# Joint stores in the last batch, a deferred matmul in its first block product, and a wider spread of the second batch's row transposes

## The chip, the core and the metric

The kernel runs on one core of one Trainium2 chip. Five engines work side by side, each through its own instruction stream: TensorE (PE, matmuls and transposes; its weight loads are listed as PEld), VectorE (DVE), ScalarE (ACT), GpSimd (POOL) and SyncE (SP, which here only issues DMAs). They meet through semaphores. The metric is device time in microseconds (us) of one launch, the median of several runs; lower is better.

## The reference

Retention attention with a decay per head, then a Fourier mix with a feed-forward block behind it. There are 4 batches of 768 rows, 8 heads of 64 columns (512 together), and a hidden width of 2048.

```python
gamma = 1.0 - 2.0 ** (-5.0 - np.arange(H, dtype=np.float32))
for t in range(S):
    state = gamma[None, :, None, None] * state + np.einsum('bhd,bhe->bhde', k[:, :, t], v[:, :, t])
    y[:, :, t] = scale * np.einsum('bhd,bhde->bhe', q[:, :, t], state)
...
X = np.fft.fft(x, axis=1)
X = np.fft.fft(X, axis=2)
u = x + np.real(X).astype(np.float32)
mu = np.mean(u, axis=-1, keepdims=True)
var = np.mean((u - mu) ** 2, axis=-1, keepdims=True)
un = (u - mu) / np.sqrt(var + 1e-06)
ch = np.maximum(un @ w_ch1, 0.0) @ w_ch2
return (u + ch).astype(np.float32)
```

## The kernel before

The batches are numbered 0 to 3. Each goes through the same stages. Attention works on pairs of heads: casts of q, k and v on POOL (`cast_unit`, L378 to L393), transposes of q and k, a masked product `wkA` (L605), the states `wkK` (L624, whose matmuls read the cast v that L393 writes), and the output `wkY` (L655, L659). The Fourier mix has two steps: `s1_unit` (L741, evicted by ACT at L748 and reversed by DVE at L752) and `s2_unit`. `s2_unit(b, kb)` makes one block `kb` of 128 rows (0 to 5) of `u`: four short matmuls into a tile `pq` (L838), two copies on ACT (L840, L841), two operations on DVE (L845, L848), two additions on POOL (L875, L877). `norm_unit` takes the row statistics on DVE (L895, L896). In batches 0 to 2 ACT then writes the centred rows `un` in half precision (L900), and the scale 1/sqrt(var) is applied behind the second matrix (`rstd_unit`, L932 and L934). In batch 3 `root_unit` (ACT, L910) and `scaled_unit` (DVE, L917, L918) write the fully normalised rows. `unT_unit` transposes `un`: for batch 0 and the first three row blocks of batch 1 on PE through PSUM (L945, evicted at L950 by DVE or at L952 by ACT), for all later ones by a DMA transpose that SP issues (L941). The tile `un` has two buffers, so the third row block's `un` takes the buffer of the first.

The feed-forward block of batches 1 and 2 works on halves of three row blocks: 16 units `h_unit` (four matmuls of 384 columns each, L961; evicted by ACT at L965 or DVE at L967 as `ACT_ROWS` says) give the hidden rows, and three `ch_unit` of 16 matmuls of 512 columns (L1000) give the result, which DVE finishes at L1004 and SP stores at L1008. Both take their PSUM tiles from a pool of three (`ps_pm`); nearly everything else takes them from a pool of five (`ps_g`).

The last batch is done in three groups `p` of two row blocks. In each, eight `h3_unit` (L1043) make the hidden rows of 256 rows, two hidden blocks n and n+8 per unit, evicted by ACT (L1048) or, for n = 4, DVE (L1050). Then `p3_unit` makes the second matrix product by blocks with seven products instead of eight, each of eight matmuls (f = 0 to 7) of 256 columns (L1107). Product 1 (bank "a") is copied by ACT into `w` (L1118); product 2 is accumulated on top of it in the same bank. Products 5, 6, 7 and 3 read sums of hidden blocks (`hsum`, four DVE operations at L1067 behind units n = 3 and n = 7). Both f = 7 of product 1 and f = 7 of product 4 read what the unit n = 7 wrote. `PROD` gives the order of the products, one for groups 0 and 1 and one for group 2. The results go to two tiles `ob` of a pool of three, and each is stored with a DMA of its own.

What sets the order: `streams` is a list of (units, start, end) with times in batches, `emit` spaces each list evenly and sorts all units by due time. Below time 3.0 the program is handed to a scheduler that may reorder within limits; above it the order is pinned as written. Due times of the first three row blocks of the next batch come from `DA0` (after batch 0) and `DA1`: entries 2 and 3 are for the `s2_unit` list, entries 4 and 5 for the `unT_unit` list. For batch 3 `mix_units` puts `norm_unit`, `root_unit` and `scaled_unit` behind each `s2_unit` in one list of 12.

Of the kernel before, what the change touches and what calls it, by code (L numbers as in the profile page):

```python
# [13 lines left out]
f32 = mybir.dt.float32  # L14
# [4 lines left out]
P = 128  # L19
B, H, S, D = 4, 8, 768, 64  # L20
DM = 512
DFF = 2048
NCH = S // P
# [9 lines left out]
DM0, DM1 = (0.120, 0.208, 0.265, 0.344), (0.004, 0.137, 0.232, 0.341)  # L33
TS0 = (0.249, 0.368, 0.406, 0.410, 0.479, 0.544, 0.680, 0.685)
TS1 = (-0.040, -0.020, 0.048, 0.585)
DA0, DA1 = (0.068, 0.080, 0.173, 0.203, 0.315, 0.321), (0.063, 0.067, 0.063, 0.158, 0.168, 0.189)
LD0, LD1 = (0.172, 0.226), (-0.370, 0.140)
HT0 = (0.655, 0.675, 0.673, 0.628)
NPE = 2
# [1 line left out]
        (0.345, 0.415, 0.435, 0.460, 0.500))  # L41
WS = (0.6, 0.97)
H3_ACT = (0, 1, 2, 3, 5, 6, 7)
PROD = ((1, 4, 2, 5, 6, 7, 3), (1, 4, 6, 7, 5, 2, 3))
HS_AT = {3: (0, 4), 7: (4, 8)}
ACT_ROWS = ((2, 5, 6, 7, 8, 9, 10, 14), (0, 3, 6, 7, 9, 10, 11, 12, 14, 15))

# [2 lines left out]
def kernel(  # L50
# [9 lines left out]
    nc = tc.nc  # L60
# [3 lines left out]
    def pool(name, bufs, **kw):  # L64
        return ctx.enter_context(tc.tile_pool(name=name, bufs=bufs, **kw))
# [11 lines left out]
    up = pool("up", 2)  # L77
    qnp = pool("qnp", 1)
    hp_ = pool("hp", 1)
    obp = pool("obp", 3)  # L80
    stt = pool("stt", 2)
    ps_g = pool("ps_g", 5, space=PSUM)
    first = ExitStack()
# [14 lines left out]
    last = const.tile([P, 4], f32, tag="last")  # L98
# [894 lines left out]
    def ch_unit(b, rt, rb3, part):  # L993
        def run():
            rb = rt * 3 + rb3
            if part == 0:
                psc_of[0] = ps_pm.tile([P, DM], f32, tag="pm", name="psc")
            psc = psc_of[0]
            for fb in range(4 * part, 4 * part + 4):
                nc.tensor.matmul(psc, ht16[:, fb, rb3 * P:(rb3 + 1) * P], w216[:, fb, :],  # L1000
                                 start=(fb == 0), stop=(fb == NFB - 1))
            if part == 3:
                ob = obp.tile([P, DM], f32, tag="ob", name="ob")
                nc.vector.scalar_tensor_tensor(out=ob, in0=psc, scalar=lb[b]["st"][:, rb, 3:4],  # L1004
                                               in1=lb[b]["u"][:, rb, :], op0=ALU.mult,
                                               op1=ALU.add)
                for c0, c1 in ((0, 256), (256, DM)) if b == 0 else ((0, DM),):
                    nc.sync.dma_start(out[b, rb * P:(rb + 1) * P, c0:c1], ob[:, c0:c1])  # L1008
        return run

    def wsum_unit(j, hi):
# [22 lines left out]
    ws, pr, hs = {}, {}, {}  # L1034
# [35 lines left out]
    def p3_unit(p, n):  # L1070
        def run():
            u = lb[B - 1]["u"]
            r0, r1 = 2 * p, 2 * p + 1
            u11, u12 = u[:, r0, 0:256], u[:, r0, 256:DM]
            u21, u22 = u[:, r1, 0:256], u[:, r1, 256:DM]
            end = p == 2
            if n == 1:
                pr.clear()
                pr["o"] = [obp.tile([P, DM], f32, tag="ob", name="ob") for _ in range(2)]
                pr["w"] = inp.tile([P, 2, NCH, D], f32, tag="in32", name="ws32").rearrange(  # L1080
                    "p a c d -> p (a c d)")[:, 0:256]
            o0, o1 = pr["o"]
            o11, o12, o21, o22 = o0[:, 0:256], o0[:, 256:DM], o1[:, 0:256], o1[:, 256:DM]
            w = pr["w"]
            bank, first, last, lh, rh = {
                1: ("a", True, False, lambda f: ht16[:, f, 0:P], lambda f: w216[:, f, 0:256]),
                2: ("a", False, True, lambda f: ht16[:, 8 + f, 0:P],
                    lambda f: w216[:, 8 + f, 0:256]),
                3: ("d", False, True, lambda f: hs[3][:, f], lambda f: w216[:, 8 + f, 256:DM]),
                4: ("e", True, True, lambda f: ht16[:, 8 + f, P:256], lambda f: wsum(3, f)),  # L1090
                5: ("d", True, False, lambda f: hs[0][:, f], lambda f: wsum(0, f)),
                6: ("b", True, True, lambda f: hs[1][:, f], lambda f: wsum(1, f)),
                7: ("c", True, True, lambda f: hs[2][:, f], lambda f: wsum(2, f))}[n]
            cols = ((0, 128), (128, 256)) if bank == "d" and end else ((0, 256),)
            if first:
                pr[bank] = [ps_g.tile([P, 256], f32, tag="g", name="psc", padded_shape=[P, DM])
                            for _ in cols]

            def add(o, x, y):
                nc.vector.tensor_tensor(out=o, in0=x, in1=y, op=ALU.add)  # L1100

            def store(r, c0, c1, src, queue=nc.sync):
                queue.dma_start(out[B - 1, r * P:r * P + P, c0:c1], src)

            for ps, (c0, c1) in zip(pr[bank], cols):
                for f in range(8):
                    nc.tensor.matmul(ps[:, c0:c1], lh(f), rh(f)[:, c0:c1],  # L1107
                                     start=first and f == 0, stop=last and f == 7,
                                     skip_group_check=True)
                if n == 3:  # L1110
                    add(o12[:, c0:c1], ps[:, c0:c1], u12[:, c0:c1])
                    if end:
                        store(r0, 256 + c0, 256 + c1, o12[:, c0:c1], nc.sync if c0 else nc.scalar)
                elif n == 5:
                    add((o22 if end else u22)[:, c0:c1], ps[:, c0:c1], u22[:, c0:c1])
            ps = pr[bank][0]
            if n == 1:
                nc.scalar.copy(w, ps)  # L1118
            elif n == 2:
                add(o11, ps, u11)  # L1120
                if end:
                    store(r0, 0, 256, o11)
            elif n == 4:
                add(u21, ps, u21)
            elif n == 6:
                add(w, ps, w)
                if end:
                    add(u22, u22, w)
                    nc.gpsimd.tensor_tensor(out=u21, in0=u21, in1=w, op=ALU.add)
                else:  # L1130
                    x = u[:, r1].rearrange("p (t m) -> p t m", t=2)
                    nc.gpsimd.tensor_tensor(out=x, in0=x, in1=w.unsqueeze(1).to_broadcast(
                        [P, 2, 256]), op=ALU.add)
                nc.gpsimd.tensor_tensor(out=u12, in0=u12, in1=w, op=ALU.add)
            elif n == 7:
                add(u22 if end else o22, ps, u22)
                add(o21, ps, u21)
                if end:
                    store(r1, 0, 256, o21)
                else:  # L1140
                    store(r1, 0, DM, o1)
            if n == 3 and not end:
                store(r0, 0, DM, o0)
            elif n == 5 and end:
                store(r1, 256, DM, o22)
        return run
# [100 lines left out]
    def mix_units(b, kbs):  # L1247
        s2s = [s2_unit(b, kb) for kb in kbs]
        if b == B - 1:
            s2s = [u for kb, s2 in zip(kbs, s2s) for u in (  # L1250
                s2, norm_unit(b, kb), root_unit(kb), scaled_unit(kb))]
        return s2s, [unT_unit(b, kb) for kb in kbs]

# [23 lines left out]
    streams = []  # L1277
    for b in range(B):
# [19 lines left out]
        if b < B - 1:  # L1298
            s2s, unTs = mix_units(b, [3, 4, 5])
# [7 lines left out]
        if b + 1 < B:  # L1307
            steps = attn_steps(b + 1)
            if b == 0:
                streams.append(([load_unit(1, i, 6) for i in range(4)], LD0[0], LD0[1]))  # L1310
                streams.append(([qt_zeros], 0.1, 0.15))
                streams.append(([half_tables], HT0[0], HT0[1]))
                streams.append(([pad_unit], HT0[2], HT0[3]))
                ts = TS0
            else:
                streams.append(([load_unit(b + 1, i) for i in range(4)], b + LD1[0], b + LD1[1]))
                n = [len(u) for u in steps[1:]]
                ts = list(TS1[:2]) + [TS1[2] + TS1[3] * sum(n[:j]) / sum(n) for j in range(6)]
            streams.append((steps[0], b + ts[0], b + ts[1]))
            streams += [(u, b + ts[j + 2], b + ts[j + 3]) for j, u in enumerate(steps[1:])]  # L1320
            end = b + ts[-1]
            da = DA0 if b == 0 else DA1
            streams.append(([s1_unit(b + 1, e, cb) for cb in range(2) for e in range(2)
                             if cb or b + 1 >= FB], end + da[0], end + da[1]))
            s2s, unTs = mix_units(b + 1, [0, 1, 2])
            streams += [(s2s, end + da[2], end + da[3]), (unTs, end + da[4], end + da[5])]
            if b + 1 == B - 1:
                streams.append(([wsum_unit(j, hi) for j in range(4) for hi in range(2)],
                                b + WS[0], b + WS[1]))
# [31 lines left out]
```

## Time and profile before

| what | value |
|---|---|
| median of 3 runs (lowest, highest) | 245.66 us (245.02, 246.42) |
| the profiled execution's own time | 245.43 us |
| span of its instructions | 243.4 us |
| what lies around the span | 2.03 us |
| PE busy, share of the span | 231.2 us, 95% |
| DVE busy | 192.5 us, 79% |
| ACT busy | 126.7 us, 52% |
| POOL busy | 87.7 us, 36% |
| granted PE clock in every stretch | 1.00 |
| last matmuls, modelled end | 240.15 us |

The page of the profile is read from the top: busy times, then the span in slices, then the chain of waits that ended last. The timeline lists instructions in order of time: start, duration, engine, source line, operation, output and inputs, shapes, count, and in brackets how long the engine stood idle before it and what ended that. Rows of the same kind that follow each other are merged, so a row `x8` covers eight instructions. Starts of matmuls are measured and their ends are modelled: two matmuls overlap in the list by some 0.2 us, and a stall shorter than that shows only as a longer distance from start to start. Those distances are therefore what the text works with.

### The profile page before, as it was taken

How to read it: one execution, taken by the hardware profiler on the slowest of the kernel's cores; microseconds unless marked ns; L12 is line 12 of the kernel's file. 1: busy time of each engine (PE TensorE's matmuls, PEld its weight loads, DVE VectorE, ACT ScalarE, POOL GpSimd, SP SyncE). 2: the span in 40 equal slices, each digit the busy share in tenths (PEclk: the TensorE clock that was granted, in tenths of full speed). 3: DMA queues.
4: the chain of work that ended last, by engine and by line, in shares of the span. 5: the costliest groups of instructions: out<-in, count | busy, mean ns of one | idle time of the engine just before them, and what ended most of it. 6: DMA issues, size and time to landing. Idle time of an engine off the chain costs nothing.

```text
span 243.4 us, 5668 instructions
## 1 busy us (share of the span) xinstructions
PE 231.2 (95%) x2160; PEld 155.6 (64%) x2160; DVE 192.5 (79%) x478; ACT 126.7 (52%) x280; POOL 87.7 (36%) x150
## 2 busy tenths in 40 slices
PE   5798899999999998999999999999999999999994
PEld 2354668956676655665567546565567458888884
DVE  8998957897797888996887777899986846776274
ACT  8798669588675434652237523741247306253330
POOL 7776601465600057791000554680002402330302
PEclk9999999999999999999999999999999999999999
DMA  7999999699989768997999767887100231131202
GB/s 171 253 264 147 195 203 205 154 252 231 287 188 226 134 142 163 166 208 114 247 284 214 163 120 222 126 112 170 67 22 0 46 109 43 24 109 24 86 3 88
DMA packets 100363, 36.41 MB, mean 150 GB/s; under 512 B 89968, under 2 KB 98288, under 8 KB 100336
## 3 DMA queue, kind: packets, MB, share of 16 engines
q1 hardware_dynamic: 95968, 31.79, 62.3%
q0 software_dynamic: 4224, 4.19, 10.7%
q8 instruction: 17, 0.28, 0.5%
q14 instruction: 10, 0.08, 0.1%
q10 hardware_dynamic: 144, 0.07, 0.1%
HBM read 27.26 MB, written 6.29 MB: 138 GB/s over the span
## 4 chain that ended last, share of the span: by engine, by line
PE 71%; DMA 7%; ACT 7%; DVE 6%; SPq 4%; POOL 2%; issue 2%; ACTq 0%; POOLq 0%; DVEq 0%
PE psc L1000 21%; PE psh L961 19%; PE psh L1043 9%; PE psc L1107 8%; DMA k<-in_k_dram 5%; SPq L171 4%; PE wkA L605 3%; PE ps L741 3%; DMA q<-in_q_dram 2%; PE wkY L659 2%; PE pq L838 2%; PE wkY L655 1%; ACT un L891 1%; PE wkK L624 1%; DVE bst L895 1%
## 5 line engine op out<-in xcount | busy, mean ns | idle before, releaser
L1000 PE MATMUL psc<-w,ht 128*128 128x512 f16 x288 | 68.2, 379 | 0.0
L961 PE MATMUL psh<-unT,w 128*128 128x384 f16 x320 | 59.7, 326 | 0.0
L875 POOL TENSOR_TENSOR u<-u,x 128x256 f32<-128x256 f32 x21 | 13.4, 637 | 105.6 <-DVE u L845 97.4
L1000 PEld LDWEIGHTS <-ht 128*128 128x128 f16 x288 | 27.2, 98 | 26.1 <-issue 0.2
L961 PEld LDWEIGHTS <-w 128*128 128x128 f16 x320 | 29.8, 98 | 15.9 <-issue 0.7
L965 ACT ACTIVATE ht<-psh 128x384 f16<-128x384 f32 x46 | 22.3, 490 | 23.6 <-PE psh L961 23.3
L608 DVE TENSOR_TENSOR atm<-wkA,maskp 128x512 f16<-128x512 f32 x36 | 23.8, 682 | 1.4 <-PE wkA L605 1.4
L1043 PE MATMUL psh<-unT,w 128*128 128x256 f16 x192 | 21.5, 273 | 0.0
L895 DVE BATCH_NORM_STATS2 bst<-u 128x6 f32<-128x512 f32 x21 | 14.6, 694 | 7.0 <-POOL u L877 6.5
L1043 PEld LDWEIGHTS <-w 128*128 128x128 f16 x192 | 18.7, 98 | 2.2
L967 DVE TENSOR_SCALAR ht<-psh 128x384 f16<-128x384 f32 x34 | 18.6, 548 | 1.8 <-PE psh L961 1.7
L1048 ACT ACTIVATE ht<-psh 128x512 f16<-128x512 f32 x21 | 12.5, 597 | 13.6 <-PE psh L1043 7.9
L634 DVE SCALAR_TENSOR_TENSOR s<-s,gk,wkK 128x128 f16<-128x128 f16 x48 | 16.4, 341 | 3.0 <-ACT s L630 2.2
L1004 DVE SCALAR_TENSOR_TENSOR ob<-psc,stats,u 128x512 f32<-128x512 f32 x18 | 13.4, 743 | 5.8 <-PE psc L1000 5.8
L900 ACT ACTIVATE un<-u,stats 128x512 f16<-128x512 f32 x15 | 10.8, 722 | 12.1 <-DVE stats L896 7.9
L667 ACT ACTIVATE x<-wkY,gexp 128x384 f16<-128x384 f32 x24 | 12.8, 581 | 8.0 <-PE wkY L659 8.0
L388 POOL TENSOR_SCALAR kd<-k,gexp 128x384 f16<-128x384 f32 x24 | 13.9, 588 | 4.3 <-DMA k<-in_k_dram 4.3
L157 PE MATMUL wps<-ht 128*128 128x512 f16 x40 | 12.6, 418 | 2.2 <-POOL ht L208 2.2
L877 POOL TENSOR_TENSOR u<-u,x 128x256 f32<-128x256 f32 x21 | 13.5, 644 | 3.0 <-DVE stats L896 3.0
L605 PE MATMUL wkA<-qTz,kT 128*128 128x256 f16 x72 | 13.4, 272 | 0.1
L840 ACT COPY qn<-pq 128x128 f32<-128x128 f32 x18 | 4.9, 273 | 14.2 <-PE pq L838 14.2
L978 PE MATMUL psh<-unT,w 128*128 128x128 f16 x192 | 11.5, 219 | 0.1
(189 smaller groups left out, 421.2 us busy)
## 6 DMA issues: line engine op xcount, KB each, us to landing
q<-in_q_dram SPq DMA_DIRECT2D x16, 384.0 KB, 6.0
k<-in_k_dram SPq DMA_DIRECT2D x16, 384.0 KB, 5.6
v<-in_v_dram SPq DMA_DIRECT2D x16, 384.0 KB, 6.2
w<-in_moe_w_ch_dram POOLq DMA_DIRECT2D x8, 512.0 KB, 11.0
out_dram<-ob SPq DMA_DIRECT2D x16, 256.0 KB, 2.4
out_dram<-ob SPq DMA_DIRECT2D x15, 128.0 KB, 1.9
unT<-un SPq DMA_TRANSPOSE x15, 2.4
qTz<-q16z SPq DMA_TRANSPOSE x8, 4.5
```

Source lines behind the costliest of these rows:

```text
L388: kc = nc.gpsimd.tensor_scalar(out=kd[:, :, h2, :], in0=k32[:, h2], scalar1=gkd[:, h0 + h2:h0 + h2 + 1], scalar2=1.0, op0=ALU.mult, op1=AL ...
L605: mm = nc.tensor.matmul(wk[:, c2], st["kT"][:, c, :], st["qT"][:, :, c, :], start=True, stop=True)
L608: nc.vector.tensor_tensor(out=st["atm"][:, 2 * part:2 * part + 2], in0=wk, in1=maskp[:, PAIR_ORDER[i]].unsqueeze(1).to_broadcast([P, 2, 2, ...
L634: nc.vector.scalar_tensor_tensor(out=s16[:, c], in0=s16[:, c - 1], scalar=gk2[:, hp:hp + 1], in1=wk[:, c - c0], op0=ALU.mult, op1=ALU.add)
L877: nc.gpsimd.tensor_tensor(out=u[:, kb, 256:512], in0=u[:, kb, 256:512], in1=x[:, kb, 1, 257:1:-1], op=ALU.add)
L895: nc.vector.bn_stats(bst, u[:, kb, :])
L961: nc.tensor.matmul(psh, w116[:, cb, fb * P:(fb + 1) * P], unT[:, cb, rt * 384:(rt + 1) * 384], start=(cb == 0), stop=(cb == 3))
L965: nc.scalar.activation(ht16[:, fb, :], psh, AF.Relu, bias=0.0, scale=-1.0)
L967: nc.vector.tensor_scalar(out=ht16[:, fb, :], in0=psh, scalar1=-1.0, scalar2=0.0, op0=ALU.mult, op1=ALU.max)
L1000: nc.tensor.matmul(psc, ht16[:, fb, rb3 * P:(rb3 + 1) * P], w216[:, fb, :], start=(fb == 0), stop=(fb == NFB - 1))
L1043: nc.tensor.matmul(psh[:, t], w116[:, cb, fb * P:(fb + 1) * P], unT[:, cb, p * 256:(p + 1) * 256], start=(cb == 0), stop=(cb == 3))
L1107: nc.tensor.matmul(ps[:, c0:c1], lh(f), rh(f)[:, c0:c1], start=first and f == 0, stop=last and f == 7, skip_group_check=True)
```

## The change

There are four edits.

1. `DA0`: the transposes of batch 1's first three row blocks are due from 0.292 to 0.326 instead of 0.315 to 0.321 behind the attention's end.
2. `mix_units` for batch 3 puts three empty units ahead of its list, and the list's end is moved so that the spacing stays; each unit of batch 3's first three row blocks is due three places later.
3. `p3_unit`: for product 1 only f = 0 to 6 are made at first; f = 7 is kept as a function and made just ahead of f = 7 of product 4, with the copy to `w` behind it. `PROD` for groups 0 and 1 takes product 5 ahead of product 2.
4. Results of the last batch go to one tile `o32` of 6 row blocks, in the pool and under the tag of `u`; groups 0 and 1 store both row blocks with one DMA at the end of product 3 (before: one after product 7, one after product 3). Batch 0's results, stored before as two halves of 256 columns, are stored with one DMA per row block.

```diff
-DA0, DA1 = (0.068, 0.080, 0.173, 0.203, 0.315, 0.321), (0.063, 0.067, 0.063, 0.158, 0.168, 0.189)
+DA0, DA1 = (0.068, 0.080, 0.173, 0.203, 0.292, 0.326), (0.063, 0.067, 0.063, 0.158, 0.168, 0.189)
...
-PROD = ((1, 4, 2, 5, 6, 7, 3), (1, 4, 6, 7, 5, 2, 3))
+PROD = ((1, 4, 5, 2, 6, 7, 3), (1, 4, 6, 7, 5, 2, 3))
...
-                for c0, c1 in ((0, 256), (256, DM)) if b == 0 else ((0, DM),):
-                    nc.sync.dma_start(out[b, rb * P:(rb + 1) * P, c0:c1], ob[:, c0:c1])
+                nc.sync.dma_start(out[b, rb * P:(rb + 1) * P, :], ob)
...
             if n == 1:
-                pr.clear()
-                pr["o"] = [obp.tile([P, DM], f32, tag="ob", name="ob") for _ in range(2)]
+                if p == 0:
+                    pr["o"] = up.tile([P, NCH, DM], f32, tag="u32", name="o32")
...
-            o0, o1 = pr["o"]
+            o0, o1 = pr["o"][:, r0], pr["o"][:, r1]
...
+            if n == 1:
+                pr["late"] = lambda: nc.tensor.matmul(pr["a"][0], lh(7), rh(7), start=False,
+                                                      stop=False, skip_group_check=True)
             for ps, (c0, c1) in zip(pr[bank], cols):
                 for f in range(8):
-                    nc.tensor.matmul(ps[:, c0:c1], lh(f), rh(f)[:, c0:c1],
-                                     start=first and f == 0, stop=last and f == 7,
-                                     skip_group_check=True)
+                    if f < 7 or n != 1:
+                        if f == 7 and n == 4:
+                            pr["late"]()
+                            nc.scalar.copy(w, pr["a"][0])
+                        nc.tensor.matmul(ps[:, c0:c1], lh(f), rh(f)[:, c0:c1],
+                                         start=first and f == 0, stop=last and f == 7,
+                                         skip_group_check=True)
...
-            if n == 1:
-                nc.scalar.copy(w, ps)
-            elif n == 2:
+            if n == 2:
...
-                else:
-                    store(r1, 0, DM, o1)
             if n == 3 and not end:
-                store(r0, 0, DM, o0)
+                nc.sync.dma_start(out[B - 1, r0 * P:r0 * P + 256].rearrange(
+                    "(r p) m -> p r m", p=P), pr["o"][:, r0:r0 + 2])
...
-            s2s = [u for kb, s2 in zip(kbs, s2s) for u in (
+            s2s = [lambda: None] * 3 + [u for kb, s2 in zip(kbs, s2s) for u in (
                 s2, norm_unit(b, kb), root_unit(kb), scaled_unit(kb))]
...
-            streams += [(s2s, end + da[2], end + da[3]), (unTs, end + da[4], end + da[5])]
+            streams += [(s2s, end + da[2], end + da[2] + (da[3] - da[2]) * len(s2s) / (
+                3 if b + 1 < B - 1 else 12)), (unTs, end + da[4], end + da[5])]
```

## The prediction

> **What bounds the kernel now.** First the page: the busy times (PE 231.2 of 243.4), then its summary of the chain that ended last.
>
> ```profile
> PE 71%; DMA 7%; ACT 7%; DVE 6%; SPq 4%; POOL 2%; issue 2%; ACTq 0%; POOLq 0%; DVEq 0%
> ```
>
> PE is busy nearly throughout, and the chain runs along it from about 61 us to 240 us. No matmul is added or removed, so the change can only win what PE loses standing still. I went through the distances of matmul starts in the timeline and found three places that the edits touch. The first is the hand-over from batch 0 to batch 1 (timeline, start and duration in us):
>
> ```profile
> 93.06 0.30 ACT L932 ACTIVATE stats<-stats,epsT 128x3 f32<-128x3 f32 x1 [0.79 <-DVE stats L896]
> ...
> 93.33 0.61 PE L945 MATMUL pst<-ident,un 128*128 128x128 f16 x8
> ...
> 93.83 0.72 ACT L900 ACTIVATE un<-u,stats 128x512 f16<-128x512 f32 x1 [0.47 <-PE pst L945]
> 94.15 0.83 POOL L393 TENSOR_SCALAR v<-v 128x768 f16<-128x768 f32 x1
> ...
> 94.61 0.40 PE L945 MATMUL pst<-ident,un 128*128 128x128 f16 x4 [0.67 <-ACT un L900]
> 94.84 0.40 PE L838 MATMUL pq<-gk,g16r 128*128 128x129 f16 x4
> 95.08 0.44 PE L624 MATMUL wkK<-v,kd 128*128 128x128 f16 x5
> ```
>
> Eight transposes take 0.44 (93.33 to 93.77), and the next four start at 94.61: 0.84 lost. `un` of the third row block (L900) waits in turn for the first block's transposes, whose buffer it takes. The second place is batch 3's first `s2_unit`, in batch 2's time:
>
> ```profile
> 184.99 0.63 PE L838 MATMUL pq<-gk,g 128*128 128x129 f16 x3
> ...
> 185.33 0.11 PEld L838 LDWEIGHTS <-g 128*128 128x128 f16 x2 [0.32 <-ACT g L748]
> ...
> 185.46 0.65 PE L961 MATMUL psh<-unT,w 128*128 128x384 f16 x3
> ...
> 186.00 0.98 PE L961 MATMUL psh<-unT,w 128*128 128x384 f16 x5
> ```
>
> From 184.99 to 186.00 lie four pq matmuls (0.24, as the unit at 188.34 with its successor at 188.58) and three L961 (0.65 per four in the chain, so 0.49): 0.73 of work in 1.01, so 0.28 lost to ACT's copies of `g`. The third place is product 1 of the last batch, in groups 0 and 1:
>
> ```profile
> 207.04 1.03 PE L1107 MATMUL psc<-w,ht 128*128 128x256 f16 x8
> ...
> 220.40 1.20 PE L1107 MATMUL psc<-w,ht 128*128 128x256 f16 x8
> ...
> 221.30 1.75 PEld L1107 LDWEIGHTS <-ht 128*128 128x128 f16 x17 [0.26 <-ACT ht L1048]
> 221.43 1.04 PE L1107 MATMUL psc<-wsum,ht 128*128 128x256 f16 x8
> ```
>
> Group 0 needs 0.87 from product 1 (207.04) to product 4 (207.91), group 1 needs 1.03; group 2 repeats it (233.68 to 234.71). So 0.16 is lost twice, waiting for the unit n = 7.
>
> **Part 3, the deferred matmul.** In the built program PE makes 7 + 7 matmuls, then the deferred one, then product 4's last. ACT ends the n = 7 eviction 0.86 after product 1 starts (220.66 + 0.60 against 220.40); the first matmul that reads it now comes after 14 x 0.109 = 1.52. That wait is gone in groups 1 and 2; in group 0 there was none. What is late next is the copy to `w`: it moves from the end of product 1 to about 1.63 + 0.24 = 1.87 behind its start and ends at 2.24. Product 2 overwrites that bank at 24 x 0.109 = 2.61 in groups 0 and 1 because product 5 now stands between; in group 2 the sum with `w` follows product 6, which ends at 2.61 + 0.17. Product 5's first reading of n = 7's `hsum` comes at 20 x 0.109 = 2.18, and that sum is ready at 221.71 - 220.40 = 1.31. Gain **0.32**, bounds 0 (something else ends at the same time) and 0.32.
>
> **Part 2, three places later.** PE now makes two h units between the last L741 and the first pq, 1.30 of work, while ACT's last copy of `g` is done 0.80 after L838's old start (183.65 + 2.14). The stall of 0.28 goes. New order behind: two h units, pq, two h units, pq, one h unit, pq, L1000. Each h unit waits for an eviction that I placed by hand: the tightest is L1000, which takes the tile of the fourth h unit. That unit ends at 187.81, ACT evicts it from about 188.0 to 188.5, and PE comes to L1000 at 188.9. Gain **0.28**, bounds 0.28 and a loss (rival three). The DMA transposes of batch 3's rows go out later; their cover is worked out there.
>
> **Part 1, transposes spread.** PE now makes 24 L1000 (from 87.29, 0.216 each, to 92.47), eight transposes (to 92.91), the last four L1000 (to 93.77), then the four late transposes. The `un` they need is bound by ACT alone: L932 starts at 93.06 because the third row's statistics end at 93.02, it takes 0.30, L900 0.72, and PE follows 0.06 later as now (94.55 to 94.61): 94.14, against 94.61. So 0.37 of the stall stays. Behind stand four pq matmuls (0.24 with the 0.23 of transposes: 94.61) and L624, which reads the cast v that POOL ends at 94.15 + 0.83 = 94.98. PE waits there 0.41 to 95.02, where it now arrives at 95.08 and never notices. Then five L624 (0.28) and the whole next `s2_unit`'s four pq (0.24) bring L961 to 95.54, against 95.52 now. What is won is three pq matmuls (0.17) that today stand behind 20 L961 and then stand ahead of them. Against this DVE's order changes: L895 of the fourth row block, which waits for POOL, now stands ahead of the second h unit's eviction L967. I get that eviction at 97.66 to 98.2, and the fifth h unit, which takes its tile, would start at 98.15: about 0.10 lost. Net gain **0.05**. Upper bound: if L624 does not wait, L961 is bound by DVE's L950 (PSUM transposed at 94.55, DVE busy with L1004 to 94.65, 0.41, PE 0.05 later: 95.11 to 95.13): 0.39 + 0.17 = 0.56. Lower bound: one h unit's time (0.65) of further stall behind L895: -0.55.
>
> [...]
>
> **Part 4, stores and buffer: 0.** The joint store of group 0 leaves at the old second store's time (215.25); the next DMA on SP, a row transpose at 215.63 that landed at 218.04, is needed by group 2 at 226.67: 8.6 of cover. Group 1's leaves near 228.2; two stores took 2.0 to 2.3 us each there, so it lands by 232.6 at the worst, and the next store is at 238.68. `o32` takes batch 2's `u`, last read by L1004 at 199.79 + 0.75, first written near 210. Batch 0's six stores save SP 0.42 each; SP's rows there wait for DVE's results, and no PE wait of 60 to 180 us in the list of waits names a DMA. Bounds: -0.2 (one longer transfer ahead of a load) to +0.4 (one issue).
>
> **Sum.** 0.32 + 0.28 + 0.05 = 0.65. The profiled execution took 245.43 (243.4 and 2.03 around it): 244.78. It lies 0.23 below the median of the runs, on whose footing this is 245.01. I give 244.9.
>
> **Rivals.**
> 1. *The spread pays all that its rows allow.* 0.32 + 0.28 + 0.56 = 1.16: **244.3**. For it: POOL's spans are the roughest of the profile, so 94.98 may not be where L624 is released. Against it: L624 does wait for L393's semaphore, and its first start, 95.08, is just behind 94.98.
> 2. *The stalls only move.* Evictions on DVE and ACT end just as late and PE meets them a unit further on: **245.5**. For it: PE lost another 1.2 in small gaps from 96 to 182, each on another engine. Against it: in part 3 I find nothing within 0.3 of the freed matmuls.
> 3. *Batch 3's rows come too late for group 0; slower.* DVE runs in order, and in the new order the second row block's L918 stands behind the third block's L895, which waits for POOL, and behind an L1004. I get: first block's `un` done 191.9 (now 191.5), second 195.6 (now 192.9), its transpose issued 195.64 behind the store of 195.2, landed 2.4 later at 198.0. PE needs it at 199.5 (now 199.82): 1.5 of cover where there were 4.4. From a second `un` later than 197.1 each us costs one us. If each of the six waits of DVE in that stretch is 0.6 longer (L895's own 0.69 is the nearest row), it is 3.6 later and costs 2.1: 245.43 - 0.65 + 2.1 = **246.9**.
>
> **Chances.** Forecast 0.44 (own range 244.3 to 245.4), rival one 0.31, two 0.12, three 0.13. I call 0.5%, 1.23 us, what a measurement here can tell from no change: below 244.43 is faster, above 246.89 slower. Rival one lies at the edge and counts 0.23 as faster; the forecast gives 0.09 of its 0.44 and rival two 0.01: 0.33. Slower: most of rival three and the worst of part 1, 0.11. Same: 0.56. Range: 243.9 (rival one, less the 0.4 by which single runs differ) to 246.1 (part 1 at its lower bound with 0.4, and part of rival three).
>
> **What would show it.** Part 3: from the first L1107 to product 5 16 x 0.109 = 1.74 in every group, and no PEld wait for `ht` L1048. Part 2: L961 directly behind the last L741, no wait for `g` L748, L1000 some 0.3 sooner; against it a PE wait at the first L1043. Part 1: two short waits, at the last transposes for L900 and at L624 for POOL L393, in place of one of 0.84. If L624 shows no wait, rival one is right; if PE's gaps between 95 and 102 grow past 0.3, or a DMA ends PE's wait at the first L1043, the forecast is wrong.

## The result and the profile after

| | before | after |
|---|---|---|
| median (lowest to highest) of 10 runs each | 245.55 us (245.02 to 246.42) | 244.35 us (243.97 to 245.25) |
| profiled execution, its span | 245.43, 243.4 us | 244.00, 241.8 us |
| last matmul's start, from there to the end of the span | 239.93, 3.50 us | 238.75, 3.07 us |

The ratio is 0.9957 with a 95% interval of 0.9941 to 0.9973, which is 1.06 us (0.66 to 1.45) less. The forecast was 244.9 in a range of 243.9 to 246.1. The time lies in the range, half a microsecond below the number. By the ratio it is on the side of "no change", but only just: 0.5% less than the median of the ten runs would be 244.32, and the 244.43 that the prediction took from its three runs lies above the 244.35. The question is therefore where 0.4 to 0.5 us come from that the sum of 0.65 does not have.

The page of the changed kernel, its row of busy times and its chain by engine:

```profile
PE 230.9 (95%) x2160; PEld 155.8 (64%) x2160; DVE 193.0 (80%) x478; ACT 126.5 (52%) x280; POOL 87.1 (36%) x150
...
PE 76%; DVE 6%; SPq 4%; POOL 4%; DMA 3%; ACT 3%; issue 2%; POOLq 0%; ACTq 0%
```

PE has the same 2160 matmuls and is busy for nearly the same time; the span is shorter because PE stands still less and because less time follows its last matmul. The first place, the hand-over from batch 0 to batch 1, in the timeline of the changed kernel (start, duration, engine, line, operation, and in brackets the idle time ahead and what ended it):

```profile
92.06 0.61 PE L945 MATMUL pst<-ident,un 128*128 128x128 f16 x8
...
92.51 1.03 PE L1000 MATMUL psc<-w,ht 128*128 128x512 f16 x4
...
92.88 0.71 ACT L900 ACTIVATE un<-u,stats 128x512 f16<-128x512 f32 x1
...
93.64 0.40 PE L945 MATMUL pst<-ident,un 128*128 128x128 f16 x4
93.75 0.83 POOL L393 TENSOR_SCALAR v<-v 128x768 f16<-128x768 f32 x1
...
93.87 0.39 PE L838 MATMUL pq<-gk,g16r 128*128 128x129 f16 x4
...
94.63 0.44 PE L624 MATMUL wkK<-v,kd 128*128 128x128 f16 x5 [0.37 <-POOL v L393]
...
94.91 0.40 PE L838 MATMUL pq<-gk,g16r 128*128 128x129 f16 x4
...
95.14 2.11 PE L961 MATMUL psh<-unT,w 128*128 128x384 f16 x12
```

The four L1000 now stand between the transposes. In place of one stall of 0.84 there are two: the last transposes wait for ACT's L900 until 93.64, and L624 waits for POOL's L393, which ends at 94.58, until 94.63. By distances from start to start, less what a matmul of that width takes, they are 0.27 and 0.53, and one of 0.07 follows ahead of the L961 at 97.81; before it was 0.84 and, ahead of the first L961, 0.11.

The second place, batch 3's first `s2_unit`:

```profile
183.90 0.67 PE L741 MATMUL ps<-ssp,ee 128*128 128x193 f16 x6
...
184.41 1.46 PE L961 MATMUL psh<-unT,w 128*128 128x384 f16 x8
...
185.71 0.40 PE L838 MATMUL pq<-gk,g 128*128 128x129 f16 x4
...
185.94 1.46 PE L961 MATMUL psh<-unT,w 128*128 128x384 f16 x8
```

Two hidden units (1.30) now follow the last L741, and the first pq starts at 185.71 with no wait for `g`. The third place, product 1 of group 1:

```profile
219.53 0.93 PE L1113 MATMUL psc<-w,ht 128*128 128x256 f16 x7
...
220.29 0.93 PE L1113 MATMUL psc<-wsum,ht 128*128 128x256 f16 x7
...
221.06 0.27 PE L1105 MATMUL psc<-w,ht 128*128 128x256 f16 x1
...
221.28 1.04 PE L1113 MATMUL psc<-wsum,hsum 128*128 128x256 f16 x8
...
221.41 0.37 ACT L1112 COPY ws<-psc 128x256 f32<-128x256 f32 x1 [1.02 <-PE psc L1105]
```

Seven, seven, the deferred one and the last of product 4; from the first matmul to product 5 it is 1.75 (1.74 in group 0; in group 2 product 6 is the next one, and it follows at 1.75).

**Where the 1.6 us of span went.** Comparing the two traces by the distances of matmul starts, and by the stretch behind the last one:

| place | before | after | less by |
|---|---|---|---|
| 56 and 61 us, L561 and L605, batch 1's first transposes | 0.194 + 0.561 | 0.180 + 0.166 | 0.41 |
| 93 to 98 us, part 1 | 0.839 + 0.114 | 0.267 + 0.531 + 0.074 | 0.08 |
| 146 us, a hidden unit | 0.089 | under 0.04 | 0.09 |
| 185 us, part 2 | 0.285 | none | 0.285 |
| 221 and 234 us, part 3 | 0.150 + 0.150 | none | 0.30 |
| from the last matmul's start to the end | 3.50 | 3.07 | 0.43 |

The three parts that the prediction worked out give 0.665 together, against 0.65. Three rows were not in it: 0.41 at 56 to 61 us, where PE's order is the same in both kernels, 0.43 behind the last matmul, and 0.09 at 146 us. The experiments were about these.

### The profile page after: what moved, and what is told of

It is laid out like the page before. It is cut to its first block, busy times and chain, and to the rows that moved or that the text cites. A ratio compares the mean times of both kernels' runs of the same rounds, so it can differ in the third digit from the quotient of the medians.

```text
span 241.8 us, 5656 instructions
## 1 busy us (share of the span) xinstructions
PE 230.9 (95%) x2160; PEld 155.8 (64%) x2160; DVE 193.0 (80%) x478; ACT 126.5 (52%) x280; POOL 87.1 (36%) x150
## 4 chain that ended last, share of the span: by engine, by line
PE 76%; DVE 6%; SPq 4%; POOL 4%; DMA 3%; ACT 3%; issue 2%; POOLq 0%; ACTq 0%
PE psc L1000 22%; PE psh L961 19%; PE psh L1042 9%; PE psc L1113 7%; SPq L171 4%; PE ps L741 4%; PE wkA L605 3%; DMA q<-in_q_dram 3%; PE psh L978 3%; PE wkY L659 2%; PE wkY L655 2%; PE pq L838 1%; PE wkK L624 1%; PE tq L561 1%; POOL u L877 1%
## 5 line engine op out<-in xcount | busy, mean ns | idle before, releaser
L1000 PE MATMUL psc<-w,ht 128*128 128x512 f16 x288 | 68.3, 379 | 0.0
L961 PE MATMUL psh<-unT,w 128*128 128x384 f16 x320 | 59.5, 326 | 0.0
L1000 PEld LDWEIGHTS <-ht 128*128 128x128 f16 x288 | 27.1, 98 | 25.7 <-issue 0.2
L961 PEld LDWEIGHTS <-w 128*128 128x128 f16 x320 | 29.9, 98 | 16.0 <-issue 0.6
L967 DVE TENSOR_SCALAR ht<-psh 128x384 f16<-128x384 f32 x34 | 18.7, 549 | 2.1 <-PE psh L961 2.1
L895 DVE BATCH_NORM_STATS2 bst<-u 128x6 f32<-128x512 f32 x21 | 14.6, 693 | 7.2 <-POOL u L877 7.1
L1042 PEld LDWEIGHTS <-w 128*128 128x128 f16 x192 | 18.7, 98 | 2.2
L667 ACT ACTIVATE x<-wkY,gexp 128x384 f16<-128x384 f32 x24 | 12.8, 581 | 8.3 <-PE wkY L659 8.3
L900 ACT ACTIVATE un<-u,stats 128x512 f16<-128x512 f32 x15 | 10.8, 721 | 10.6 <-DVE stats L896 7.1
L388 POOL TENSOR_SCALAR kd<-k,gexp 128x384 f16<-128x384 f32 x24 | 13.9, 590 | 3.8 <-DMA k<-in_k_dram 3.8
L605 PE MATMUL wkA<-qTz,kT 128*128 128x256 f16 x72 | 13.4, 273 | 0.1
L978 PEld LDWEIGHTS <-w 128*128 128x128 f16 x192 | 11.0, 98 | 0.7 <-issue 0.5
```

Source lines behind the costliest of these rows:

```text
L605: mm = nc.tensor.matmul(wk[:, c2], st["kT"][:, c, :], st["qT"][:, :, c, :], start=True, stop=True)
L895: nc.vector.bn_stats(bst, u[:, kb, :])
L961: nc.tensor.matmul(psh, w116[:, cb, fb * P:(fb + 1) * P], unT[:, cb, rt * 384:(rt + 1) * 384], start=(cb == 0), stop=(cb == 3))
L967: nc.vector.tensor_scalar(out=ht16[:, fb, :], in0=psh, scalar1=-1.0, scalar2=0.0, op0=ALU.mult, op1=ALU.max)
L978: mm = nc.tensor.matmul(psh[:, f], w116[:, cb, fb * P:(fb + 1) * P], unT[:, cb, kb * P:(kb + 1) * P], start=(cb == 0), stop=(cb == 3))
L1042: nc.tensor.matmul(psh[:, t], w116[:, cb, fb * P:(fb + 1) * P], unT[:, cb, p * 256:(p + 1) * 256], start=(cb == 0), stop=(cb == 3))
```

## The experiments

### Each part alone on the kernel before

Four kernels ran on one chip and share 35 runs of the kernel before (median 245.49). The deferred matmul with the new order of products:

```diff
-PROD = ((1, 4, 2, 5, 6, 7, 3), (1, 4, 6, 7, 5, 2, 3))
+PROD = ((1, 4, 5, 2, 6, 7, 3), (1, 4, 6, 7, 5, 2, 3))
...
+            if n == 1:
+                pr["late"] = lambda: nc.tensor.matmul(pr["a"][0], lh(7), rh(7), start=False,
```

> The kernel before with the deferred matmul and the order of products alone. My theory (term 0.32): the two stalls of 0.15 at product 1 of groups 1 and 2 are gone, all else as before, so 0.3 us less. Rival (the stalls only move): they come back at product 5 or at the copy's bank and the time stays. Third theory, for the 0.4 us that the changed kernel has gained already at 62 us: if that gain is chance in the landing of batch 1's loads, the stall at 61 us lies anywhere from 0.1 to 0.6 us here too, though nothing ahead of 200 us is changed.

Measured: 245.15, ratio 0.9989 (0.9974 to 1.0004), 0.27 us less. Both stalls of 0.15 are gone and none comes up in their place. At 56 and 61 us the stalls are 0.62 and 0.09.

Batch 3's units three places later:

```diff
-            s2s = [u for kb, s2 in zip(kbs, s2s) for u in (
+            s2s = [lambda: None] * 3 + [u for kb, s2 in zip(kbs, s2s) for u in (
```

> The kernel before with batch 3's first units three places later alone. My theory (term 0.28): the stall of 0.285 at 185 us is gone and no new one over 0.1 us lies between 183 and 210, so 0.28 us less. Rival three (rows too late for group 0): a DMA ends PE's wait at the first matmuls of group 0, and the time grows by up to 2 us. The stall at 61 us as in the run of the deferred matmul: by chance, or 0.56 as before if it belongs to the program.

Measured: 244.93, ratio 0.9979 (0.9963 to 0.9994), 0.52 us less. The 0.285 is gone and no stall over 0.1 us lies between 183 and 210. At 56 and 61 us: 0.18 and 0.33. The 0.089 at 146 us is 0.06 here, and 0 to 0.06 in all the other profiles, with the change's parts or without, so it is not the change either.

The wider spread of the transposes:

```diff
-DA0, DA1 = (0.068, 0.080, 0.173, 0.203, 0.315, 0.321), (0.063, 0.067, 0.063, 0.158, 0.168, 0.189)
+DA0, DA1 = (0.068, 0.080, 0.173, 0.203, 0.292, 0.326), (0.063, 0.067, 0.063, 0.158, 0.168, 0.189)
```

> The kernel before with the wider spread of batch 1's transposes alone. My theory (term 0.05): the stall of 0.84 to 0.95 at 93 us falls apart into about 0.27 at the last transposes (ACT L900) and 0.5 at L624 (POOL L393), and 0.05 to 0.1 us is won. Rival one: no wait at L624 and 0.56 us won. Third theory: PE's lead at 92 us over the kernel before, if any, comes from the loads alone and not from this edit.

Measured: 245.09, ratio 0.9976 (0.9964 to 0.9989), 0.59 us less, which looks like rival one. But the trace shows the two short stalls that my theory expects, 0.254 and 0.532, with 0.075 behind them: 0.09 won at the place. PE even came out later than in the kernel before (last matmul's start 240.20, since it lost 0.93 at 56 and 61 us), and yet the span is shorter, 243.25: it is 3.05 from the last matmul's start to the end, in place of 3.50. So an edit at 93 us shortened the end of the program.

Batch 0's stores whole:

```diff
-                for c0, c1 in ((0, 256), (256, DM)) if b == 0 else ((0, DM),):
-                    nc.sync.dma_start(out[b, rb * P:(rb + 1) * P, c0:c1], ob[:, c0:c1])
+                nc.sync.dma_start(out[b, rb * P:(rb + 1) * P, :], ob)
```

> The kernel before with batch 0's results stored by one DMA per row block alone. My theory (term 0): no difference over 0.2 us in the time, and no PE wait from 61 to 180 us that is shorter. Rival: this edit is where the 0.4 us ahead of 75 us come from that the prediction lacks; then the stall at 61 us is 0.17 here and 0.56 in the runs without it, and 0.4 us is won. Chance: the stall at 61 us lies between 0.1 and 0.6 with no regard to the edit.

Measured: 245.22, ratio 0.9989 (0.9975 to 1.0004), 0.27 us less. The stalls at 56 and 61 us are 0.16 each, as in the changed kernel and as the rival has it. One run cannot tell that from chance.

### The end of SP's stream

What the last drains do is not in the timeline, but their events are in the trace. SP's instructions of these profiles, counted from 0, with start and idle time ahead (us):

```
                      no. 79                no. 207
before         95.19  idle 0.43      DRAIN  242.54  idle 0.36   of 211
e1_late        95.12  idle 0.43      DRAIN  242.07  idle 0.34   of 211
e2_three_later 95.19  idle 0.43      DRAIN  242.19  idle 0.36   of 211
e3_spread      95.60  idle 0.43      EVENT  242.86  idle 0.37   of 210
e4_whole_st.   97.44  idle 0.44      there is none              of 205
after          97.46  idle 0.43      there is none              of 201
```

SP stands still ahead of its instruction number 207, whichever that is, and also ahead of number 79, which is 128 earlier. In the kernel before, number 207 is the second of SP's last drains, for which all engines wait: 0.36 there against 0.06 in the changed kernel. The spread alone has one wait on a semaphore less on SP, so that the pause falls one instruction later, beside POOL's own last steps. Ten instructions less (eight DMAs and two waits) leave none with that number. Of the 0.43, 0.30 is this pause; the drain behind it took 0.12 in place of 0.01, and 0.02 is left over. The kernel with whole stores has no pause, yet its end takes 3.43: there the last store's semaphore is third in the list of nine that SP waits for at the end, and six waits at 0.06 follow it; in the changed kernel it is the last of the list.

The test is an edit that takes SP instructions away and does nothing to PE, the joint stores alone:

```diff
-                pr.clear()
-                pr["o"] = [obp.tile([P, DM], f32, tag="ob", name="ob") for _ in range(2)]
+                if p == 0:
+                    pr["o"] = up.tile([P, NCH, DM], f32, tag="u32", name="o32")
...
-                store(r0, 0, DM, o0)
+                nc.sync.dma_start(out[B - 1, r0 * P:r0 * P + 256].rearrange(
+                    "(r p) m -> p r m", p=P), pr["o"][:, r0:r0 + 2])
```

> The kernel before with the joint stores and their one buffer in the last batch alone. My prediction's term: 0. New theory (the end of SP's stream): in the kernel before, with the deferred matmul and with the later units SP stands still for 0.36 us between its last two drains, ahead of its instruction number 207 counted from 0, out of 211; with the spread (210 instructions) the same 0.36 lies one instruction later, and in the changed kernel (201) it is not there. Here SP has 207 instructions, so none is number 207: from the last matmul's start to the end of the span 3.05 to 3.2 us instead of 3.50, and 0.3 to 0.4 us less time, with PE's stalls as before (0.15 twice at product 1, 0.285 at 185 us, 0.84 at 93 us). Rival: the pause belongs to something else in the end, and the 3.50 stay.

Measured: 245.20 against 245.67, ratio 0.9986 (0.9973 to 0.9998), 0.34 us less. The pause is gone and the end takes 3.19, since two waits now follow the last store's; PE's stalls of 0.838, 0.282 and twice 0.151 are all there. My term of 0 for this part was wrong, and not for a reason in the stores.

The opposite edit adds SP instructions, so that number 207 moves away from the drains by another road:

```diff
-                for c0, c1 in ((0, 256), (256, DM)) if b == 0 else ((0, DM),):
+                for c0, c1 in (((0, 128), (128, 256), (256, DM)) if b == 0 else
+                               ((0, 256), (256, DM)) if b == 1 and rb < 2 else ((0, DM),)):
```

> The kernel before with eight more store DMAs: batch 0's rows in three pieces instead of two, the first two row blocks of batch 1 in two instead of one. End theory: SP has 217 instructions, number 207 falls into the waits for the landing of the last stores, where 0.36 us lie beside a wait that is there anyway; from the last matmul's start to the end 3.05 to 3.15 us instead of 3.50 and 0.4 us less time, although SP issues more. My prediction's reckoning (0.42 of SP's time saved per store that falls away, hidden): no change, or slower by up to 0.4. Theory that stores of batch 0 set the stall at 61 us: that stall is 0.56 or more.

Measured: 247.78, ratio 1.0085 (1.0064 to 1.0106), 2.1 us more. The end behaves as expected: number 207 is now one of the waits for the last stores, with its 0.36, and the stretch from the last matmul is 3.06. But all that I said of the time is wrong. PE has new stalls of 0.93, 0.22 and 0.84 between 116 and 123 us, and one of 0.33 at 222.6. In the timeline of this kernel there:

```profile
112.14 3.71 SPq L941 DMA_TRANSPOSE unT<-un  x2
...
116.59 0.72 ACT L900 ACTIVATE un<-u,stats 128x512 f16<-128x512 f32 x1 [5.66 <-DMA unT<-un]
...
117.93 0.65 PE L624 MATMUL wkK<-v,kd 128*128 128x128 f16 x5 [0.77 <-ACT x L667]
...
119.37 1.47 SPq L553 DMA_TRANSPOSE qTz<-q16z  x1
...
123.35 0.38 PE L605 MATMUL wkA<-qTz,kT 128*128 128x256 f16 x2 [0.67 <-DMA qTz<-q16z]
```

SP's row transposes (L941) go out at 112 us; in the kernel before two of the three left from 103.95 on. ACT stands 5.66 us for the buffer `un` that they free, with L667 and so PE's L624 behind it. In the kernel before, ACT also waited for this buffer, less than half as long, and PE did not notice:

```profile
108.06 0.72 ACT L900 ACTIVATE un<-u,stats 128x512 f16<-128x512 f32 x1 [2.15 <-DMA unT<-un]
```

The added issues by themselves are the smaller part of the delay: from 92 to 112 us two more stores leave than in the kernel before, 0.85 of SP's time. Most of it is SP's order in this build. In the kernel before, the two L941 stand ahead of the third pair of L553 and L555; here that pair (4.7 us) stands ahead of them, and three loads (3.4) in place of two (1.0). Some of these issues also take longer here (this L553 3.45, in the kernel before 1.45), and the runs do not show why. So this run confirms the account of the end, but what a further store costs by itself it does not show.

### The stalls at 56 and 61 us

The changed kernel with batch 0's stores in halves again:

```diff
-                nc.sync.dma_start(out[b, rb * P:(rb + 1) * P, :], ob)
+                for c0, c1 in ((0, 256), (256, DM)) if b == 0 else ((0, DM),):
+                    nc.sync.dma_start(out[b, rb * P:(rb + 1) * P, c0:c1], ob[:, c0:c1])
```

> The changed kernel with batch 0's stores in halves again. Theory that whole stores shorten the stalls at 56 and 61 us (0.32 and 0.35 together with them, 0.51 to 0.93 in the four runs without): those stalls are 0.5 or more here, and the time is 0.3 to 0.4 us above the changed kernel. Theory of chance in the landing of batch 1's loads: the sum lies anywhere from 0.3 to 0.9. End theory: SP has 206 instructions, no pause of 0.36 at the end, the time within 0.15 of the changed kernel.

Measured: 244.59, ratio 0.9958 (0.9942 to 0.9974), the changed kernel's own. The stalls are 0.127 and 0.244, less than the theory of the stores allows, and SP's end has no pause (206 instructions, 3.17). The changed kernel itself, profiled once more:

> The changed kernel once more, beside the next run on one chip. Theory of chance in the landing of batch 1's loads: the sum of the stalls at 56 and 61 us, 0.35 in the first profile, is any number from 0.3 to 0.95 here. End theory: again 3.05 us from the last matmul's start to the end of the span. Stalls of 0.27 and 0.53 at 93 us as before, ratio to the kernel before 0.994 to 0.997.

Measured: 244.44, ratio 0.9957 (0.9942 to 0.9972), stalls 0.158 and 0.471, 3.07 at the end. The sums at 56 and 61 us over the runs that leave the loads alone, the one with more stores (1.31) aside: 0.37, 0.51, 0.71, 0.76, 0.79, 0.93 with batch 0's stores in halves and 0.32, 0.35, 0.56, 0.63, 0.92 with whole ones. They overlap, and the changed kernel alone has given 0.35 and 0.63; the 0.41 between the first two profiles is within what one kernel gives by chance. What sets them is when batch 1's k lands, and with it POOL's L388, as the next edit shows.

The loads wait for the last matmul of a chosen hidden unit of batch 0 (the first load then leaves at 44.6 us). One unit earlier:

```diff
-            if (kb, g) == (1, 3):
+            if (kb, g) == (1, 2):
                 lb[0]["mm"] = mm
```

> The changed kernel with batch 1's loads tied to the hidden unit one before (kb 1, g 2 in place of g 3), so that they go out at about 43.7 in place of 44.58 us. Theory of chance in the landing of the loads: the stalls at 56 and 61 us, whose sum was 0.32 to 0.93 in the runs that issued the first load at 44.3 to 44.7, fall to the 0.3 that were their least, and the median falls by 0.1 to 0.4 us below the changed kernel's, ratio to the kernel before 0.994 to 0.9955. Rival: the transfers share the DMA engines with the last weights until 45.1 us, land no sooner, and ratio and stalls are as in the changed kernel.

Measured: 243.86, ratio 0.9948 (0.9933 to 0.9963). The first load goes out at 43.64, and the sum of the two stalls is 0.18. In the changed kernel (timeline, POOL's cast of k and the transposes that read it):

```profile
60.15 1.15 POOL L388 TENSOR_SCALAR kd<-k,gexp 128x384 f16<-128x384 f32 x2 [1.84 <-DMA k<-in_k_dram]
...
61.35 0.34 PEld L561 LDWEIGHTS <-kd 128*128 128x128 f16 x6 [0.17 <-POOL kd L388]
```

and with the loads sooner:

```profile
58.56 1.15 POOL L388 TENSOR_SCALAR kd<-k,gexp 128x384 f16<-128x384 f32 x2 [0.83 <-DMA k<-in_k_dram]
...
61.08 0.38 PEld L561 LDWEIGHTS <-kd 128*128 128x128 f16 x6
```

The cast ends 1.4 us ahead of the transposes instead of at them. The same kernel once more, beside the changed one on the same chip:

> The changed kernel with batch 1's loads tied one hidden unit sooner, once more, beside the changed kernel itself. If the gain of the first run is real: no stall at 61 us, 0.2 at most at 56 us, and 0.2 to 0.5 us below the median of the changed kernel on the same chip. Rival: the first run was lucky, and both stand at the same median within 0.15.

Measured: 244.05 against 244.44, ratio to the kernel before 0.9940 (0.9924 to 0.9956); stalls 0.18 and none. This version is the fastest of the study by its medians. The intervals of the two ratios overlap, but on this chip all five of its runs (243.83 to 244.07) lie below all ten of the changed kernel (244.15 to 245.13).

### Part 1 by itself

The changed kernel with the transposes back at their old place:

> The changed kernel with the transposes of batch 1 where they were before. SP has 201 instructions in both, so the end is the same (3.05 us behind the last matmul's start), and what is left of the spread is its place: the stall of 0.84 at 93 us and 0.11 at 95 are back in place of 0.27, 0.53 and 0.07. End theory and the prediction's term of part 1: 0.05 to 0.1 us slower than the changed kernel (ratio 0.9957 to the kernel before, here about 0.996). Rival, that the spread by itself is worth the 0.4 to 0.6 us that the kernel with the spread alone has won: ratio about 0.998 here.

Its edit is the line of `DA0` above, the other way round. Measured: 244.30 against 245.09 on its chip, ratio 0.9970 (0.9959 to 0.9981). That lies between the two expectations, and the interval reaches to both; the trace decides. The stalls are 0.838 and 0.115 again, 0.953 against 0.872, and the end is 3.05 against 3.07: 0.08 for the place.

If POOL's L393 is all that holds L624, then holding L624 back should free PE:

```diff
-                un.append(kv_unit(b, i))
+                un.append(held(kv_unit(b, i)) if (b, i) == (2, 0) else kv_unit(b, i))
```

> The changed kernel with the first state unit of batch 2 (L624, which waits 0.53 for POOL's cast of v) held back behind the fourth hidden unit of batch 1. My theory of part 1 (its lower stall is POOL's L393 and nothing else): the 0.53 goes, the first L961 is then bound by DVE's copy L950 and starts 0.4 us sooner, and up to 0.4 us is won if the evictions of four hidden units in a row keep up; if they do not, stalls of 0.1 to 0.3 come up between 97 and 101 us. Rival: another wait of the same length stands at the first L961 and the time is that of the changed kernel.

Measured: 244.92, ratio 0.9967 (0.9951 to 0.9984): nothing won. In its timeline:

```profile
94.27 0.40 PE L945 MATMUL pst<-ident,un 128*128 128x128 f16 x4
...
94.50 0.40 PE L838 MATMUL pq<-gk,g16r 128*128 128x129 f16 x4
94.88 0.41 DVE L950 COPY unT<-pst 128x512 f16<-128x512 f16 x1
...
95.35 2.77 PE L961 MATMUL psh<-unT,w 128*128 128x384 f16 x16 [0.45 <-DVE unT L950]
```

The first L961 starts 1.08 behind the last transposes, 1.50 in the changed kernel, so it is 0.42 sooner, as I said. But PE stood 0.62 ahead of it, waiting for DVE's copy, and the five L624 and four pq matmuls (0.51) that filled that time before came later, with another stall of 0.20. Two chains end here within 0.1 of each other, POOL's cast of v and DVE's copy of `unT`; to take one of them out of the way wins nothing while PE has no other work. That was the rival.

## Why the prediction was right, and what it lacked

**Part 3, 0.32 forecast, 0.30 measured.** Only the two later groups had the stall, the deferred matmul took it out of both, and nothing came up at the product behind. The copy to `w` starts 1.88 behind product 1 (forecast 1.87), and product 5 follows at 1.74 to 1.75 (1.74).

**Part 2, 0.28 forecast, 0.285 measured.** The order is two hidden units, pq, two, pq, one, pq, as worked out. L1000 comes at 188.36 against 189.23, of which 0.58 is lead from before, so 0.29.

**Part 1, 0.05 forecast, 0.08 measured.** L624 waits for POOL, as the forecast said against rival one. The two waits came out as 0.27 and 0.53, not 0.37 and 0.41, with nearly the same sum: L900 started 0.21 behind L932 and not 0.30, so the transposes came sooner and only waited longer at L624, which POOL's end sets; the first L961 starts at 95.14 against 95.52 with a lead of 0.39 at 80 us, so just level (forecast 95.54 against 95.52). The 0.10 for the fifth hidden unit behind DVE's L895 was 0.07. That term, as rival three's, takes it that DVE does not run a ready instruction ahead of an earlier one that waits. The trace of the kernel before shows this at one place:

```profile
212.95 0.29 ACT L910 ACTIVATE stats<-stats,epsT 128x1 f32<-128x1 f32 x1 [4.42 <-DVE stats L896]
...
213.48 0.76 DVE L1100 TENSOR_TENSOR ob<-psc,u 128x256 f32<-128x256 f32 x2 [0.57 <-POOL u L1132]
...
214.15 0.15 DVE L917 RECIPROCAL stats<-stats 128x1 f32<-128x1 f32 x1
```

L917's input was there at 213.24; DVE stood idle until 213.48 for POOL and ran L917 only behind L1100. The changed kernel does not test it between L895 and L967, since L895 could start at 96.61 without a wait, when the second hidden unit's matmuls were just ending. The kernel with the held L624 shows it there:

```profile
97.24 0.69 DVE L895 BATCH_NORM_STATS2 bst<-u 128x6 f32<-128x512 f32 x1 [0.47 <-POOL u L877]
...
97.85 0.54 DVE L967 TENSOR_SCALAR ht<-psh 128x384 f16<-128x384 f32 x1
```

DVE stood idle there until 97.24 for POOL, and ran the eviction L967, whose last matmul had ended at 96.83, only behind L895.

**Rival three, slower.** The second row block's transpose went out at 194.88 and landed at 197.27; PE needed it at 198.95. That leaves 1.68 of cover where the forecast had 1.5, and 4.45 before. No wait came of it, but nearly two thirds of the cover are spent.

**Rival one.** Its time, 244.3, is close to the 244.35, but its mechanism is not there: it asked for no wait at L624.

**The step that failed** is "Part 4, stores and buffer: 0". It asked what an issue saves SP and which transfer is late, and took what lies behind the last matmul as the same in both. The stores and the buffer as such did bring nothing that the traces show. But ten instructions less on SP took a pause of 0.36 out of the closing drains, and the stretch behind the last matmul is 0.43 shorter in the profiled pair. With it the sum is 0.30 + 0.285 + 0.08 + 0.43 = 1.10, against 1.06 (0.66 to 1.45) by the ratio. The bound of +0.4 that I gave for a gain of part 4 is as large, but by luck: it stood for one store issue saved, and no such saving shows. That the time fell into the range says little about this term. The single parts win more than the whole when added up (0.27 + 0.52 + 0.59 + 0.27 + 0.34 = 1.99), one reason being that the spread and the joint stores each take the end's pause away by themselves, which can be won only once; the rest is within their intervals.

**What the chance in the loads did.** The profiled pair differs by 1.43 us, more than the medians, because the profile of the kernel before had 0.755 at 56 and 61 us and that of the changed kernel 0.346. I took the first for fixed; it is a draw from 0.3 to 0.95.

What stays open: why SP pauses at these numbers (below), and whether the spread has any worth beyond its 0.08, which the run without it could not rule out.

## What to carry to other kernels

Account for the end of the program as for any stage: which engine's closing drains and waits come last, and whether an edit changes how many instructions that engine's stream has (here ten fewer on SP took 0.36 us out). Before an edit gets the credit for a difference between two profiles, look whether the place already differs between two profiles of kernels that are the same there. And when PE waits for two engines that end together, neither is worth speeding up alone; count what work PE still has ready.

## What the hardware showed unexpectedly

SP paused ahead of the instructions number 79 and 207 of its stream, 0.43 to 0.44 and 0.34 to 0.37 us, in every profile that has an instruction of that number (all fourteen have a number 79, five a number 207), be it a DMA, a wait or a drain. In the five that have a number 207, a DMA packet of 8,192 bytes on queue q14, which the page lists as "instruction" (10 packets in the kernel before, 9 in the changed one), follows 0.6 to 1.0 us behind it, and in all fourteen one follows 0.7 to 2.3 us behind number 79. Whether these packets have to do with the pause was not shown.

The kernel with eight more store DMAs was 2.1 us slower, in the main because DMA transposes came later in SP's order. The wait for the row transposes showed on ACT first: 2.15 us for a buffer cost PE nothing in the kernel before, 5.66 did.
